# Decode attention that streams a 512 MiB K/V cache: V tiles moved to a second DMA queue, and one shared pool of buffers at the end

## The chip, the cores and the metric

One core of one Trainium2 chip runs the kernel. The metric is device time in microseconds (us), as the median of several executions. Executions of one kernel agree within about 0.1%, so differences of 2 us are readable. Profiled executions give a span that is about 1.8 us shorter than the device time of the same run (1308.8 us beside 1310.64 us for the kernel before). Times inside a trace count from the start of the span.

In the profile lines PE is TensorE, DVE is VectorE, ACT is ScalarE and SP is SyncE; SPq and ACTq are the parts of SyncE and ScalarE that issue loads. "The 16 engines" are the DMA engines that move the bytes. A load is issued when its instruction runs, and has landed when the last engine has counted up the load's semaphore. The PV product is softmax(scores) times V; an eviction is ScalarE's copy of its result from the buffer `psb` to `O_sb`.

## The reference, cut to what matters

Eight requests (B = 8) decode one token each. A gated mixture of two branches is computed:

```python
q = (x @ wq) per head                       # H = 32 heads, Dh = 128
scores = q . k_cache * Dh**-0.5             # k_cache: [8, 32, 4096, 128] bf16
o = softmax(scores) . v_cache               # v_cache: the same shape
a = o @ wo                                  # [4096, 576]
b = gelu(layernorm(x) @ w1 + b1) @ w2 + b2  # w1: [576, 4608], w2: [4608, 576]
out = g * a + (1 - g) * b                   # g: a sigmoid gate
```

The two caches are 268 MB each and every byte is read once. The four weights add 20 MB. The arithmetic on each byte is small, so this is a kernel that streams memory. The diffs and listings below are cut to their core: `...` and words in place of operands stand for what is left out.

## The kernel before

The work is cut into 64 tiles g: four heads of one request, K and V of 4 MiB each, 32 KB per partition. There are two buffers for K and two for V. One buffer `RB` holds the weights in turn: wq, then w1, then w2, then wo. Everything large is loaded from SyncE's queue, in program order:

```python
def load_k(g):                              # waits until the multiplies of tile g-2 have read the buffer
    k_land[g] = op("sync", dma KB[g % 2] <- k_cache tile g, [k_done.get(g - 2)], dma=(sK[s], ...))

def load_v(g):                              # waits until the PV product of tile g-2 has read the buffer
    t = op("sync", dma VB[g % 2] <- v_cache tile g, [v_done.get(g - 2)], dma=(sV[s], ...))
# (both abbreviated)

for g in range(NG):                         # NG = 64
    if 1 <= g <= NG - 3:
        load_k(g + 1)
    if 1 <= g <= NG - 2 and g != NG - 3:
        load_v(g)
    ...
    scores(g, between)                      # 4 chunks: VectorE multiplies K by q, TensorE sums, VectorE reduces
                                            # in chunk 3: the PV product of tile g-1 on TensorE, ScalarE evicts it
    if g == NG - 3:
        load_k(g + 2)
        load_v(g)
    ...
    if g == UP0 + UPN:  load_w2()           # g = 15; w1 is issued before the loop
    if g == DN0 + DNN:  load_wo()           # g = 25
    ...
    softmax(g)                              # ends in 4 exponentials on ScalarE
```

A K buffer is free after the fourth multiply of its tile (line `DVE p L354` in the profile). A V buffer is free one tile later, after the PV product (`PE psb L414`). The last V tile (V63) is loaded in seven pieces so that its product can start early.

## Time and profile before

| | before |
|---|---|
| median device time | 1310.35 us (3 runs, 1310.23 to 1310.52) |
| bytes moved by DMA | 557.8 MB |
| DMA rate in a steady stretch (620 to 1000 us) | 431 GB/s |
| VectorE, TensorE, ScalarE busy | 66%, 64%, 16% of the span |
| K load, issue to landing (median) | 27.2 us |
| V load, issue to landing (median) | 33.1 us |

These lines are from the profile page of the kernel before: the GB/s moved in each of 40 equal slices of the span, the main row of the DMA queue table (packets, MB, share of 16 engines' span), the chain of waits that ended last, the group of K multiplies on VectorE, and two rows of the list of DMA issues (count, KB each, us to landing).

```profile
GB/s 398 422 431 432 431 432 431 432 431 430 434 424 432 430 431 429 428 418 432 429 431 429 431 431 431 431 432 430 432 430 431 431 431 429 432 431 432 429 420 311
...
q1 hardware_dynamic: 24944, 556.95, 99.4%
...
DMA 69%; DVE 20%; PE 10%; SPq 0%; issue 0%; ACT 0%
...
L354 DVE TENSOR_TENSOR p<-KB,q_bc 128x4096 bf16<-128x4096 bf16 x256 | 579.6, 2285 | 278.0 <-DMA KB<-in_A_k_cache_dram 278.0
...
KB<-in_A_k_cache_dram SPq DMA_DIRECT2D x64, 4096.0 KB, 27.2
VB<-in_A_v_cache_dram SPq DMA_DIRECT2D x63, 4096.0 KB, 33.1
```

What to see: the rate is 429 to 434 GB/s in nearly all slices, queue 1 alone keeps the 16 DMA engines busy for 99.4% of the span, the chain is 69% DMA, and VectorE spent 278 us waiting for K tiles. This kernel is bound by its DMA engines. In the trace's packet records a 32 KB packet takes 1216 ns, and 16 engines at 32 KB per 1216 ns are the 431 GB/s. The Trainium skill, "DMA: Bandwidth & Descriptors", section "Where 436 GB/s comes from", gives 435.2 GB/s as the ceiling; this trace runs 1% below it.

### The profile page before, as it was taken

The numbers are of one execution on the slowest core, as the hardware profiler recorded it, in microseconds if no ns is written. First come the engines' busy times: TensorE is split into PE (matmuls) and PEld (weight loads), VectorE is DVE, ScalarE is ACT, GpSimd is POOL, SyncE is SP. The second block draws the span as 40 slices with busy tenths as digits, with TensorE's granted clock in tenths as the row PEclk, the third lists the DMA queues.
The fourth block names the chain that finished last, engine by engine and source line by source line (L and its number), as shares of the span: only waits on it lengthen the run. The fifth ranks groups of instructions, "written<-read, shape, count | busy, mean of one in ns | idle before, by whom it ended". The sixth has DMA issues, their size and how long they took to land.

```text
span 1308.8 us, 12641 instructions
## 1 busy us (share of the span) xinstructions
PE 843.5 (64%) x5428; PEld 384.4 (29%) x5428; DVE 869.7 (66%) x1061; ACT 204.1 (16%) x393; POOL 2.5 (0%) x13
## 2 busy tenths in 40 slices
PE   3567766766746666646766766765766665766766
PEld 1223433433312233212322222322322222322323
DVE  4576676676747667646766766766776666776675
ACT  1201111111210110101011111011111111111111
POOL 0000000000000000000000000000000000000000
PEclk8878888878868888768878878878878878878878
DMA  9999999999999999999999999999999999999997
GB/s 398 422 431 432 431 432 431 432 431 430 434 424 432 430 431 429 428 418 432 429 431 429 431 431 431 431 432 430 432 430 431 431 431 429 432 431 432 429 420 311
DMA packets 25255, 557.77 MB, mean 426 GB/s; under 512 B 2528, under 2 KB 6640, under 8 KB 7536
## 3 DMA queue, kind: packets, MB, share of 16 engines
q1 hardware_dynamic: 24944, 556.95, 99.4%
q8 instruction: 42, 0.69, 0.2%
q14 instruction: 13, 0.11, 0.0%
q10 hardware_dynamic: 256, 0.03, 0.0%
HBM read 556.96 MB, written 0.01 MB: 426 GB/s over the span
## 4 chain that ended last, share of the span: by engine, by line
DMA 69%; DVE 20%; PE 10%; SPq 0%; issue 0%; ACT 0%
DMA KB<-in_A_k_cache_dram 68%; DVE p L354 16%; PE psb L364 10%; DVE s_sb L369 3%; DMA VB<-in_A_v_cache_dram 1%; SPq L187 0%; PE psb L414 0%; ACT L467 0%; SPq L229 0%; DVE mA L387 0%; SPq L223 0%; PE psb L477 0%; DVE mB L389 0%; ACT O_sb L427 0%; DVE gm L390 0%
## 5 line engine op out<-in xcount | busy, mean ns | idle before, releaser
L364 PE MATMUL psb<-p,ident 128*128 128x512 bf16 x2048 | 610.9, 459 | 412.2 <-DVE p L354 411.8
L354 DVE TENSOR_TENSOR p<-KB,q_bc 128x4096 bf16<-128x4096 bf16 x256 | 579.6, 2285 | 278.0 <-DMA KB<-in_A_k_cache_dram 278.0
L364 PEld LDWEIGHTS psb<-p,ident 128*128 128x128 bf16 x2048 | 218.1, 114 | 744.5 <-DVE p L354 445.2
L369 DVE TENSOR_REDUCE s_sb<-psb 128x32 f32<-128x512 f32 x256 | 176.1, 688 | 129.9 <-PE psb L364 129.6
L427 ACT ACTIVATE O_sb<-psb 128x512 f32<-128x512 f32 x63 | 37.6, 597 | 1032.2 <-PE psb L414 1032.2
L396 ACT ACTIVATE P<-s_sb,mD 32x128 bf16<-32x128 f32 x256 | 147.0, 574 | 12.9 <-DVE mD L393 9.0
L414 PE MATMUL psb<-VB,P 128*16 128x512 bf16 x2016 | 119.9, 379 | 0.3 <-DMA VB<-in_A_v_cache_dram 0.3
L432 PE MATMUL psb<-sel,O_sb 128*128 128x4 f32 x504 | 66.9, 256 | 32.9 <-ACT O_sb L427 32.9
L432 PEld LDWEIGHTS psb<-sel,O_sb 128*128 128x128 f32 x504 | 61.6, 192 | 41.3 <-ACT O_sb L427 41.2
L414 PEld LDWEIGHTS psb<-VB,P 128*16 128x16 bf16 x2016 | 44.7, 89 | 70.4 <-issue 26.3
L402 DVE TENSOR_REDUCE rs<-P 128x4 f32<-128x512 bf16 x64 | 43.5, 680 | 2.1 <-ACT P L396 2.1
L421 PEld LDWEIGHTS psb<-rs,ones 128*128 128x128 f32 x128 | 24.4, 192 | 9.3 <-issue 0.4
L348 ACT ACTIVATE q_bc<-psb 128x128 bf16<-128x128 f32 x64 | 17.4, 272 | 32.7 <-PE psb L346 32.7
L452 PEld LDWEIGHTS psb<-yT_sb,RB 128*128 128x128 bf16 (+1 forms) x216 | 19.4, 165 | 3.4
L452 PE MATMUL psb<-yT_sb,RB 128*128 128x8 bf16 (+1 forms) x216 | 19.8, 227 | 0.0
L387 DVE TENSOR_REDUCE mA<-s_sb 128x1 f32<-128x128 f32 x64 | 18.3, 286 | 2.2
L421 PE MATMUL psb<-rs,ones 128*128 128x4 f32 x128 | 18.4, 214 | 0.0
L389 DVE STREAM_TRANSPOSE mB<-mA 128x32 f32<-128x32 f32 x64 | 13.6, 213 | 2.2
L393 DVE STREAM_TRANSPOSE mD<-mC 128x32 f32<-128x32 f32 x64 | 13.6, 212 | 2.2
L346 PE MATMUL psb<-Q,Sel 128*128 128x128 bf16 x64 | 14.7, 229 | 0.0
L346 PEld LDWEIGHTS psb<-Q,Sel 128*128 128x128 bf16 x64 | 6.1, 96 | 27.0 <-issue 26.8
L390 DVE TENSOR_REDUCE gm<-mB 128x1 f32<-128x32 f32 x64 | 11.9, 186 | 2.2
(63 smaller groups left out, 84.7 us busy)
## 6 DMA issues: line engine op xcount, KB each, us to landing
KB<-in_A_k_cache_dram SPq DMA_DIRECT2D x64, 4096.0 KB, 27.2
VB<-in_A_v_cache_dram SPq DMA_DIRECT2D x63, 4096.0 KB, 33.1
RB<-in_B_w_dram SPq DMA_DIRECT2D x1, 5184.0 KB, 44.3
RB<-in_B_w_dram SPq DMA_DIRECT2D x1, 4608.0 KB, 36.6
RB<-in_A_wo_dram SPq DMA_DIRECT2D x1, 4608.0 KB, 44.7
RB<-in_A_wq_dram SPq DMA_DIRECT2D x1, 4096.0 KB, 12.8
VB<-in_A_v_cache_dram SPq DMA_DIRECT2D x2, 1024.0 KB, 8.7
VB<-in_A_v_cache_dram SPq DMA_DIRECT2D x3, 512.0 KB, 11.2
```

Of the source, the lines that this page charges most:

```text
L346: t = op("tensor", lambda e: e.matmul(qb_ps[:, 0:DH], lhsT=Sel[:, b, :], rhs=Q4[:, hg * DH:(hg + 1) * DH], start=True, stop=True), [a_Q[hg ...
L354: v_mult[g, c] = op("vector", lambda e: e.tensor_tensor(out=p1[:, par, :, :], in0=KB[s][:, c * CT:(c + 1) * CT, :], in1=qb, op=ALU.mult), ...
L364: p_sum[g, c] = op("tensor", lambda e, r=r, n=n: e.matmul(tr_ps[par][:, :], lhsT=ident[:, :], rhs=r, start=(n == 0), stop=(n == NCH - 1)), w)
L369: v_red[g, c] = op("vector", lambda e: e.tensor_reduce(out=s_sb[:, s, c * CT:(c + 1) * CT], in_=tr_ps[par][:, :].rearrange("p (t c) -> p t ...
L387: t = op("vector", lambda e: e.tensor_reduce(out=mA[:, 0:1], in_=s_sb[:, s, :], axis=AX.X, op=ALU.max), [v_red[g, NCK - 1], c_mA])
L396: a_exp[g] = op("scalar", lambda e, h=h, q=q: e.activation(out=P[q, s, :, h], in_=s_sb[q, s, :], func=ACT.Exp, bias=mD[q, s, 0:1], scale=1.0),
L402: v_rs[g] = op("vector", lambda e: e.tensor_reduce(out=rs[:, s, :], in_=P[:, s, :, :].rearrange("p t h -> p h t"), axis=AX.X, op=ALU.add), ...
L414: p_pv[g] = op("tensor", lambda e, o=o, tq=tq: e.matmul(o, lhsT=P[:, s, tq * TQ:(tq + 1) * TQ, :].rearrange("p t h -> p (t h)"), rhs=VB[s] ...
L421: p_z[g] = op("tensor", lambda e: e.matmul(oz_ps[:, HB:2 * HB], lhsT=ones[:, :], rhs=rs[:, g % 2, :], start=True, stop=True), [v_rs[g], v_ ...
L427: a_ev[g] = op("scalar", lambda e: e.activation(out=O_sb[:].rearrange("p t d -> p (t d)"), in_=o_ps[s][:, :], func=ACT.Copy), [p_pv[g], p_ ...
L432: p_oz[g] = op("tensor", lambda e, tt=tt: e.matmul(oz_ps[:, 0:HB], lhsT=O_sb[:, tt, :], rhs=sel16[:, tt, :], start=(tt == 0), stop=(tt == ...
L452: st["p_up"] = op("tensor", lambda e, w=w, o=o, kt=kt: e.matmul(o, lhsT=w, rhs=yT_sb[:, kt, :], start=(kt == 0), stop=(kt >= NKF)), [*ld_w ...
```

## The change

Its intent: let a V and a K tile be in flight together from two queues, so that one queue's wait for a free buffer never holds up the other, and bring V63 and K63 forward at the end by letting them use whichever of the four buffers is free first. The diff, cut to its core:

```diff
-    KB = [sb(f"KB{i}", [128, NTT, DH], BF16) for i in range(2)]
-    VB = [sb(f"VB{i}", [128, NTT, DH], BF16) for i in range(2)]
+    KV = [sb(f"KV{i}", [128, NTT, DH], BF16) for i in range(4)]
...
+    k_slot = {g: g % 2 for g in range(NG)}
+    v_slot = {g: 2 + g % 2 for g in range(NG)}
+    k_slot[NG - 1], v_slot[NG - 3], v_slot[NG - 1] = 3, 1, 0
+    free = [None] * 4
...
+    def load_tile(cache, g, i, engine="sync"):
+        nS[i] += 1
+        src = kv_src(cache, g)
+        return op(engine, lambda e: e.dma_start(KV[i][:, :, :], src), [free[i]], dma=(sS[i], 16 * nS[i]))
...
     def load_v(g):
-        ... op("sync", ...)
+        v_land[g] = [(load_tile(A_v_cache, g, v_slot[g], "scalar" if 1 <= g < NG - 4 else "sync"), 0, NTT)]
...
     for g in range(NG):
         if 1 <= g <= NG - 3:
             load_k(g + 1)
+        if g == NG - 3:
+            load_k(g + 2)
+        if g == NG - 1:
+            load_v_pieces(g)
...
-                    pv(NG - 3, 0, 1)         # before: the pieces of V63 had to wait for this product
-                    evict(NG - 3)
-                    load_v_pieces(g)
```

So V1 to V59 are issued by ScalarE, in its program order after the exponentials of the tile before. The weights, K and the other V tiles stay on SyncE's queue.

More of the change, by code (lines that the diff above doesn't have):

```diff
@@ L180, in bass_gated_mix__mha_block_cached__mixer_channel_mlp__decode_kernel @@
     YT_COL = 64
-    sK = [nc.alloc_semaphore(f"sK{i}") for i in range(2)]
-    sV = [nc.alloc_semaphore(f"sV{i}") for i in range(2)]
-    nK, nV = [0, 0], [0, 0]
+    sS = [nc.alloc_semaphore(f"sS{i}") for i in range(4)]
+    nS = [0] * 4
+    k_slot = {g: g % 2 for g in range(NG)}
+    v_slot = {g: 2 + g % 2 for g in range(NG)}
+    k_slot[NG - 1], v_slot[NG - 3], v_slot[NG - 1] = 3, 1, 0
+    free = [None] * 4
     def load(engine, dst, src, name, waits=()):
@@ L214, in kv_src @@
         return cache[b, hg * HB:(hg + 1) * HB].rearrange("h (p t) d -> (h p) t d", p=32)
-    k_done, v_done = {}, {}
     k_land, v_land = {}, {}
+    def load_tile(cache, g, i, engine="sync"):
+        nS[i] += 1
+        src = kv_src(cache, g)
+        return op(engine, lambda e: e.dma_start(KV[i][:, :, :], src), [free[i]], dma=(sS[i], 16 * nS[i]))
     def load_k(g):
-        s = g % 2
-        nK[s] += 1
-        src = kv_src(A_k_cache, g)
-        k_land[g] = op("sync", lambda e: e.dma_start(KB[s][:, :, :], src), [k_done.get(g - 2)], dma=(sK[s], 16 * nK[s]))
+        k_land[g] = load_tile(A_k_cache, g, k_slot[g])
     def load_v(g):
-        s = g % 2
-        nV[s] += 1
-        src = kv_src(A_v_cache, g)
-        t = op("sync", lambda e: e.dma_start(VB[s][:, :, :], src), [v_done.get(g - 2)], dma=(sV[s], 16 * nV[s]))
-        v_land[g] = [(t, 0, NTT)]
+        v_land[g] = [(load_tile(A_v_cache, g, v_slot[g], "scalar" if 1 <= g < NG - 4 else "sync"), 0, NTT)]
     V_LAST = (32, 32, 16, 16, 16, 8, 8)
     def load_v_pieces(g):
-        s = g % 2
+        i = v_slot[g]
         src = kv_src(A_v_cache, g)
@@ L239, in load_v_pieces @@
         for n, nt in enumerate(V_LAST):
-            dst, part = VB[s][:, t0:t0 + nt, :], src[:, t0:t0 + nt, :]
-            t = load("sync", dst, part, f"sVl{n}", [v_done.get(g - 2)])
+            dst, part = KV[i][:, t0:t0 + nt, :], src[:, t0:t0 + nt, :]
+            t = load("sync", dst, part, f"sVl{n}", [free[i]])
             v_land[g].append((t, t0, t0 + nt))
@@ L354, in mult @@
         v_mult[g, c] = op("vector", lambda e: e.tensor_tensor(
-            out=p1[:, par, :, :], in0=KB[s][:, c * CT:(c + 1) * CT, :], in1=qb, op=ALU.mult),
+            out=p1[:, par, :, :], in0=KV[k_slot[g]][:, c * CT:(c + 1) * CT, :], in1=qb, op=ALU.mult),
             [k_land[g], a_qb[g], p_sum.get((g, c - 2) if c >= 2 else (g - 1, c + NCK - 2))]
@@ L358, in mult @@
         if c == NCK - 1:
-            k_done[g] = v_mult[g, c]
+            free[k_slot[g]] = v_mult[g, c]
         for n in range(NCH):
@@ L415, in pv @@
                     o, lhsT=P[:, s, tq * TQ:(tq + 1) * TQ, :].rearrange("p t h -> p (t h)"),
-                    rhs=VB[s][:, tq * TQ:(tq + 1) * TQ, :].rearrange("p t d -> p (t d)"),
+                    rhs=KV[v_slot[g]][:, tq * TQ:(tq + 1) * TQ, :].rearrange("p t d -> p (t d)"),
                     start=(tq < 4), stop=(tq >= NTQ - 4)), w)
-        v_done[g] = p_pv[g]
+        free[v_slot[g]] = p_pv[g]
     def total(g):
@@ L508, in pv_turned @@
                 p_oz[g] = op("tensor", lambda e, t=t: e.matmul(
-                    o_ps[s][:, 0:HB], lhsT=VB[s][:, t, :], rhs=P[:, s, t, :], start=(t == 0), stop=(t == NTT - 1)),
+                    o_ps[s][:, 0:HB], lhsT=KV[v_slot[g]][:, t, :], rhs=P[:, s, t, :], start=(t == 0), stop=(t == NTT - 1)),
                     [land, a_exp[g], a_ev.get(g - 2)] if t == t0 else ())
@@ L539, in between @@
                     total(g - 1)
-                else:
-                    pv(NG - 3, 0, 1)
-                    evict(NG - 3)
-                    load_v_pieces(g)
             if c == 2:
@@ L555, in between @@
                     evict(g - 1)
+                if g == NG - 1:
+                    pv(g - 2, 0, 1)
+                    evict(g - 2)
                 if g == UP0 + UPN:
@@ L562, in bass_gated_mix__mha_block_cached__mixer_channel_mlp__decode_kernel @@
         if g == NG - 3:
-            load_k(g + 2)
             load_v(g)
```

## The prediction

> **What bounds it.** The DMA engines. The DMA queue table gives queue 1 556.95 MB and 99.4% of the 16 engines' span; the 40-slice strip shows DMA at 9 throughout and 429 to 432 GB/s in almost every slice; the chain of waits is 68% K loads. In the packet records a 32 KB packet takes 1216 ns (middle half 1214 to 1219), i.e. 16 x 26.95 GB/s = 431 GB/s: packets follow each other without gaps. VectorE (66%) and TensorE (64%) have room: in a pair's 19.45 us of DMA, the last multiply ends 11.7 us after its K landed.
>
> The Trainium skill, "DMA: Bandwidth & Descriptors", "Where 436 GB/s comes from", puts the ceiling at 435.2 GB/s; the trace agrees, being 1% below it. So even a perfect rate over 557 MB could save only about 12 us (estimate from that page's figure).
>
> **What the change does.**
> 1. 59 V loads (V1 to V59) move from SyncE's queue to ScalarE's. By the page's "Issuing engines are not separate DMA queues" both run on the same 16 engines. No byte and no gap between packets is there to be removed: I expect 430 to 433 GB/s in steady stretches: 0 us, perhaps -4.
> 2. ScalarE issues 59 loads at 0.33 us = 19 us, on an engine 16% busy: off the path. A V load now follows the four exponentials of the previous tile, about 3 us later than its buffer is free. At half rate a V tile takes 19.45 us, so the next V is queued before the last lands: both queues stay filled.
> 3. Transients. Where SyncE's queue holds weights ahead of K (w1 at 45 to 60 us, w2 near 330, wo near 540), V no longer waits behind them and runs two tiles ahead, worst at wo, whose 1152-byte packets (51 ns) alternate with V's 1216 ns packets if engines switch per packet. Afterwards K streams alone at 9.7 us a tile, faster than the 11.7 us that free a K buffer: 1 to 4 us of DMA idleness each, estimate +5 us in all.
> 4. End. Now V63 waits for the PV product of tile 61 and is issued at 1289.5 us; the windows view shows 360, 221, 291 GB/s in 1286 to 1292 us (about 2 us of DMA time lost). With the pool, V63 goes into K62's buffer, free about 13 us earlier, so the gap disappears: -2 to -3 us. The tail after the last landing (about 4.1 us) stays.
>
> All DMA time, and nothing else, is on the critical path. Sum: +5 -2.5 -1.5 = +1 us. I predict **1310 us, range 1301 to 1319** (8 in 10); chances: faster by over 2% 0.03, within 2% 0.93, slower 0.04.
>
> **What would show it.** Right: queue 1 about 309 MB and queue 10 about 247 MB, summing in time to nearly the whole span; steady windows at 431 GB/s; K's median issue-to-landing still about 27 us, V's up from 33 to 36 to 40 us; no dip below 380 GB/s before the last 8 us; short dips near 95, 350 and 575 us; VectorE still waiting for K about 4 us per tile. Step 1 is wrong if steady windows leave 429 to 434; step 3 is wrong if those dips are absent; step 4 if the last 25 us still dip.
>
> **What would make it wrong.** Two interleaved streams could cost the HBM side rate (a steady 5 GB/s less is +15 us); sharing could be unfair per queue, so that K, which gates the multiplies, lands later and starves VectorE; or SyncE's blocked issue (23.6 us once, near 542 us, behind wo) could hold up ScalarE's issue and with it the exponentials.

## The result, and the profile after

The changed kernel takes 1322.97 us (median of 4 runs, 1322.59 to 1323.56), beside 1310.40 us for the kernel before in the same rounds. The ratio is 1.0096, 95% interval 1.0079 to 1.0114. A ratio here is the mean time of one kernel's runs over that of the other's of the same rounds, so it is not quite the ratio of the medians. The change made the kernel 12.6 us slower. That is within 2%, and outside the predicted range.

The same lines of the profile page, of the changed kernel (queue 10 is ScalarE's):

```profile
GB/s 398 423 373 419 435 429 427 432 434 431 434 425 392 429 428 434 432 409 365 432 436 430 428 428 436 432 431 429 431 429 431 434 430 432 429 429 433 431 434 306
...
q1 hardware_dynamic: 16448, 309.48, 54.9%
q10 hardware_dynamic: 8752, 247.50, 43.6%
...
DMA 56%; DVE 23%; PE 14%; another core or an unknown queue 6%; ACT 1%; issue 0%; SPq 0%; DVEq 0%
...
L354 DVE TENSOR_TENSOR p<-KV,q_bc 128x4096 bf16<-128x4096 bf16 x256 | 579.6, 2285 | 295.5 <-DMA KV<-in_A_k_cache_dram 289.3
...
KV<-in_A_k_cache_dram SPq DMA_DIRECT2D x64, 4096.0 KB, 27.2
KV<-in_A_v_cache_dram ACTq DMA_DIRECT2D x59, 4096.0 KB, 28.0
```

Most slices still show 427 to 435 GB/s. The lost time is local: apart from the first slices and the last, which are alike in both, slices 3 and 4 (373 and 419), 13 (392) and 18 and 19 (409 and 365) lie below the rest, where the kernel before has 431, 432, 432, 418 and 432.

The windows view shows what happens there. Its columns are the window, its length, busy time and instruction count of each engine, the granted clock, the DMA share and the GB/s. First the kernel before, then the changed one:

```profile
60.00:100.00 40.00, 22.90 (x129) 11.34 (x130) 25.06 (x26) 5.90 (x12) 0.00 (x0) 0.79 1.00 430
380.00:420.00 40.00, 26.28 (x156) 11.64 (x155) 27.74 (x33) 6.12 (x12) 0.00 (x0) 0.82 1.00 428
600.00:640.00 40.00, 25.84 (x182) 11.50 (x182) 27.15 (x33) 6.13 (x12) 0.00 (x0) 0.84 1.00 429
620.00:1000.00 380.00, 249.40 (x1508) 109.10 (x1509) 263.31 (x312) 58.21 (x114) 0.00 (x0) 0.82 1.00 431
```

```profile
60.00:94.00 34.00, 5.72 (x22) 2.71 (x22) 6.38 (x8) 3.02 (x6) 0.00 (x0) 0.55 1.03 438
94.00:99.00 5.00, 3.19 (x16) 1.43 (x15) 5.00 (x4) 0.00 (x0) 0.00 (x0) 1.00 0.05 20
99.00:104.00 5.00, 4.46 (x48) 2.18 (x47) 2.66 (x8) 1.39 (x4) 0.00 (x0) 1.00 0.89 321
402.00:408.00 6.00, 3.96 (x20) 1.83 (x19) 5.37 (x4) 0.00 (x0) 0.00 (x0) 1.00 0.69 257
614.00:620.00 6.00, 4.92 (x21) 2.04 (x19) 5.60 (x4) 0.00 (x0) 0.00 (x0) 0.87 0.13 55
700.00:1200.00 500.00, 327.67 (x1973) 143.48 (x1973) 345.47 (x410) 76.54 (x150) 0.00 (x0) 0.82 1.00 431
```

In three short stretches the changed kernel moves far less than in the others: 20 GB/s from 94 to 99 us, 257 GB/s from 402 to 408 us, 55 GB/s from 614 to 620 us. Elsewhere the rate is 431 GB/s over 500 us, as before. From the packet records, the time in which the 16 engines had no packet sums (as a mean over engines) to about 4.7, 2.6 and 4.7 us in the three stretches, 12.0 us together (12.2 us if the first and last moments of each stretch are counted in full); the kernel before has none there. At the end (from 1255 us to the last packet) the engines idle for 7.2 us after and 7.0 us before. The 12.0 us are nearly the whole difference between the two profiled spans (1321.7 - 1308.8 = 12.9 us). The median duration of a 32 KB packet is unchanged (1216 ns before; 1215 ns on either queue after), so two streams side by side cost no rate that can be seen.

Why the first stretch is idle can be read from the timeline of the changed kernel (start us, duration, engine and line, operation, count, and in brackets the idle time before and what ended it). These are the K multiplies of tile 2 and the next issues of V (ScalarE) and of K (SyncE):

```profile
56.15 0.33 SPq L224 DMA_DIRECT2D KV<-in_A_k_cache_dram  x1
```

```profile
60.12 0.33 ACTq L224 DMA_DIRECT2D KV<-in_A_v_cache_dram  x1
...
102.73 0.34 ACTq L224 DMA_DIRECT2D KV<-in_A_v_cache_dram  x1
```

```profile
87.06 4.50 DVE L354 TENSOR_TENSOR p<-KV,q_bc 128x4096 bf16<-128x4096 bf16 x2 [27.00 <-DMA KV<-in_A_k_cache_dram]
...
93.65 2.28 DVE L354 TENSOR_TENSOR p<-KV,q_bc 128x4096 bf16<-128x4096 bf16 x1
...
96.45 2.28 DVE L354 TENSOR_TENSOR p<-KV,q_bc 128x4096 bf16<-128x4096 bf16 x1
```

```profile
98.76 0.33 SPq L224 DMA_DIRECT2D KV<-in_A_k_cache_dram  x1
```

K3 was issued at 56.15 us, V2 at 60.12 us. VectorE then waited 27 us for K2, which lay in SyncE's queue behind w1, while V used the other queue: K2 landed at 87.0 us (in the kernel before, VectorE started on it at 67.9 us), and V2 had landed at 76.4 us, before it. From there both V buffers were full, and V3 could only be issued at 102.73 us, after the PV product of tile 1. So only K3 was left to move. With the engines to itself it took about 10 us and its last packet ended at 96.3 us. The next K load needs the buffer of K2, which VectorE had read by 98.76 us. Its first packet ran at 99.7 us. In between the DMA engines had nothing to do. The same pattern follows w2 and wo. After wo it is as strong: both V buffers were full at 594.5 us, the held K tile landed at 607.2 us, and the next K load was issued at 619.1 us. After w2 it is milder: the last V tile landed at 401.9 us, 6.4 us after the held K tile (395.4 us), so V had not got as far ahead. The next K load was issued at 406.8 us, before the K tile ahead of it had wholly landed (407.9 us), and the engines ran dry one after another from 404 us on; all 16 were without a packet for only 0.3 us, against 3.4 us in the first stretch and 3.6 us in the third.

### The profile page after: what moved, and what is told of

The parts are those of the page before. It is cut to its first block, busy times and chain, and to the rows that moved or that the text cites. A ratio compares the mean times of both kernels' runs of the same rounds, so it can differ in the third digit from the quotient of the medians.

```text
span 1321.7 us, 12641 instructions
## 1 busy us (share of the span) xinstructions
PE 836.4 (63%) x5428; PEld 381.3 (29%) x5428; DVE 869.5 (66%) x1061; ACT 204.2 (15%) x393; POOL 2.5 (0%) x13
## 4 chain that ended last, share of the span: by engine, by line
DMA 56%; DVE 23%; PE 14%; another core or an unknown queue 6%; ACT 1%; issue 0%; SPq 0%; DVEq 0%
DMA KV<-in_A_k_cache_dram 56%; DVE p L354 19%; PE psb L364 12%; DVE s_sb L369 4%; PE psb L414 2%; ACT O_sb L427 0%; PE psb L508 0%; ACT q_bc L348 0%; PE psb L432 0%; SPq L190 0%; ACT L467 0%; SPq L224 0%; DVE mA L387 0%; DVE rs L402 0%
## 5 line engine op out<-in xcount | busy, mean ns | idle before, releaser
L354 DVE TENSOR_TENSOR p<-KV,q_bc 128x4096 bf16<-128x4096 bf16 x256 | 579.6, 2285 | 295.5 <-DMA KV<-in_A_k_cache_dram 289.3
L414 PE MATMUL psb<-KV,P 128*16 128x512 bf16 x2016 | 119.9, 379 | 0.0
L414 PEld LDWEIGHTS psb<-KV,P 128*16 128x16 bf16 x2016 | 44.7, 89 | 69.9 <-issue 26.3
```

The costliest lines, as they stand in the source:

```text
L354: v_mult[g, c] = op("vector", lambda e: e.tensor_tensor(out=p1[:, par, :, :], in0=KV[k_slot[g]][:, c * CT:(c + 1) * CT, :], in1=qb, op=ALU ...
L414: p_pv[g] = op("tensor", lambda e, o=o, tq=tq: e.matmul(o, lhsT=P[:, s, tq * TQ:(tq + 1) * TQ, :].rearrange("p t h -> p (t h)"), rhs=KV[v_ ...
```

## The experiments

Eleven kernels were run, each timed against the kernel before in 3 rounds on the same chip. All results passed the comparison with the reference, even that of the one kernel that uses wrong rows of wo (the comparison did not notice it). "Idle" below is the mean time without a packet over the 16 engines, worked out from the packet records of the trace, in stretches apart from the start and the end.

### Which part of the change costs: the second queue or the new end?

Only the queue of V is changed in the kernel before:

```diff
-        t = op("sync", ...VB[s]..., [v_done.get(g - 2)], ...)
+        t = op("scalar" if 1 <= g < NG - 4 else "sync", ...VB[s]..., [v_done.get(g - 2)], ...)
```

> The kernel before, with one thing changed: V1 to V59 are issued from ScalarE's queue. The order at the end and the buffers stay as they were. Theory (V runs two tiles ahead while weights sit in SyncE's queue, then K alone drains its queue before a K buffer is free): the three idle stretches of the DMA engines near 95, 405 and 615 us appear as in the changed kernel, 12 us together, and the time is 1321 to 1324 us. Rival (the new order at the end, with K63 in a V buffer and V63 in a K buffer, is what costs): within 2 us of the kernel before.

Measured: 1323.23 us, ratio 1.0098 (1.0083 to 1.0113). Idle: 4.8, 3.2 and 4.9 us at the same three places.

Only the new end is kept:

```diff
-        ... "scalar" if 1 <= g < NG - 4 else "sync"
+        ... "sync"
```

> The changed kernel with every load on SyncE's queue again, so only the rearranged end of the change is left. Theory: no idle stretch outside the end; 1307 to 1311 us, since the end of the changed kernel lost as much DMA time (7.2 us) as that of the kernel before (7.0 us). Rival (the end costs): above 1315 us.

Measured: 1310.31 us, ratio 0.9999 (0.9982 to 1.0016), no idle stretch. The three windows of the kernel with only the queue changed show the idle stretches without the new end:

```profile
94.00:98.00 4.00, 3.99 (x16) 1.63 (x14) 4.00 (x3) 0.00 (x0) 0.00 (x0) 0.84 0.04 16
404.00:408.00 4.00, 2.43 (x11) 0.99 (x12) 4.00 (x4) 0.00 (x0) 0.00 (x0) 1.00 0.23 98
615.00:619.00 4.00, 2.91 (x15) 1.28 (x12) 4.00 (x3) 0.00 (x0) 0.00 (x0) 1.00 0.15 66
```

The queue costs the 12.6 us, and the end neither costs nor gains.

### Is it V running ahead, or are two streams the trouble?

V stays on ScalarE's queue, and waits one event more:

```diff
+        after_k = [k_land[g]] if engine == "scalar" else []
-        return op(engine, ..., [free[i]], ...)
+        return op(engine, ..., [free[i], *after_k], ...)
```

> The changed kernel, and each V load on ScalarE's queue also waits until the K tile of the same number has landed, so V cannot run ahead of K while weights are loaded. Both queues still run together. Theory: the three idle stretches are gone or below 1 us each, 1309 to 1312 us. Rival (two interleaved streams cost by themselves, or issuing late from ScalarE starves the DMA engines): as slow as the changed kernel, 1320 us or more, since V is now issued later still.

Measured: 1310.33 us, ratio 0.9998 (0.9983 to 1.0013). The windows that were idle are full:

```profile
94.00:98.00 4.00, 2.49 (x10) 1.14 (x10) 4.00 (x2) 1.89 (x4) 0.00 (x0) 0.66 0.96 406
404.00:408.00 4.00, 3.48 (x14) 1.57 (x13) 3.97 (x6) 0.00 (x0) 0.00 (x0) 0.76 0.95 410
615.00:619.00 4.00, 3.27 (x29) 1.43 (x30) 3.53 (x4) 0.00 (x0) 0.00 (x0) 1.00 1.02 442
```

Two queues are in use as before, and V is issued later than in the changed kernel, and still the loss is gone. So neither interleaving nor a late issue from ScalarE is the cause. The loss comes from the order in which tiles arrive: it is gone when V may not run ahead of K.

### Does it matter which stream the weights hold up?

```diff
-    ld_w1 = [load("sync", w1_sb, ...), load("sync", w1_t, ...)]
+    ld_w1 = [load("scalar", w1_sb, ...), load("scalar", w1_t, ...)]
     # likewise w2 and wo
```

> The changed kernel with w1, w2 and wo loaded from ScalarE's queue, ahead of V instead of ahead of K. Theory: K is no longer held up, so the stretches near 95 and 405 us vanish (7.3 us less); wo may block ScalarE itself, as it blocked SyncE's next issue for 35 us, and that would stop the exponentials, so its stretch may stay or grow. 1310 to 1320 us. Rival (the loads of weights cost the same wherever they are queued, because two queues share the engines): 1322 us with three stretches.

Measured: 1310.42 us, ratio 0.9999 (0.9984 to 1.0014), no idle stretch, not even the one after wo that the expectation left open. With the weights ahead of V it is V that comes late, and V has slack: a tile's product is needed only near the end of the next tile's multiplies. The feared block did occur, and cost nothing. The timeline of ScalarE in this run, around wo:

```profile
551.98 0.39 ACTq L190 DMA_DIRECT2D RB<-in_A_wo_dram  x1
...
552.52 31.87 ACTq L224 DMA_DIRECT2D KV<-in_A_v_cache_dram  x1
...
584.43 0.60 ACT L427 ACTIVATE O_sb<-psb 128x512 f32<-128x512 f32 x1 [29.49 <-issue]
```

The V load behind wo held ScalarE's queue for 31.87 us, and the eviction at 584.43 us came 29.49 us after ScalarE's last work. Enough K and V was in the queues that the DMA engines did not run dry.

### Is a whole K buffer the wait that leaves the engines idle?

V may run ahead here, but K is loaded and freed in halves:

```diff
+        k_half[g] = op("sync", dma first half of K,  [half_free[i]], dma=(sH[i], ...))   # free after multiply 1
+        k_land[g] = op("sync", dma second half of K, [free[i]], dma=(sS[i], ...))        # free after multiply 3
```

> The changed kernel with each K tile loaded as two halves of 2 MiB, each half waiting only for the multiplies that read it. V still runs ahead as in the changed kernel. The first half of a K buffer is free about 4.6 us after its K landed, sooner than the other K buffer is filled by K alone (about 8 us after). Theory (the idle stretch is K waiting for a whole buffer): no stretch over 1 us; the halves double K's packets, estimated from 32 KB at 1216 ns and 8 KB at 309 ns as 3 us more in all, so 1312 to 1315 us. Rival (V running ahead is harmful in itself, whatever K's grain): stretches as before, 1324 us or more.

Measured: 1315.06 us, ratio 1.0034 (1.0019 to 1.0049), at the top of the expected range (0.06 us above it), with no idle stretch (426, 422 and 475 GB/s in the windows at 94 to 98, 404 to 408 and 615 to 619 us). V did run ahead here: V2 landed at 83.4 us, K2 at 87.5 us. The remaining 4.5 us (against 1310.57 us for the kernel before in these rounds) fit the smaller packets: a 16 KB packet takes 614 ns, so two take 12 ns more than one of 32 KB, and the packet time summed over the run is 5.8 us per engine above that of the changed kernel (1310.2 against 1304.4 us), which more than covers them. Two things are needed for the idle stretch, then: V has run ahead, and K waits for a whole buffer. Taking away either one removes it.

### Does the size of packets decide how far V gets ahead?

wo is read as one run of 36 KB per partition, which puts the wrong rows in it (a wrong result):

```diff
-        A_wo.rearrange("(h d) n -> d h n", d=128)     # 32 runs of 1152 B per partition
+        A_wo.rearrange("(d h) n -> d h n", d=128)     # 1 run of 36 KB per partition
```

> The changed kernel with wo read as one run of 36 KB per partition in place of 32 runs of 1152 bytes: wrong result on purpose, same bytes. If the engines switch between the queues packet by packet, V is held up by wo as it is by w2 (41 KB packets, stretch 2.6 us), and the third stretch shrinks from 4.7 us to 2 to 3.5 us; with 2 us less for the larger packets the time is 1318 to 1320 us. Rival (the size of the stretch does not come from the packets' sizes): the stretch stays at 4.7 us and the time at 1320.5 to 1321.5 us.

Measured: 1319.47 us, ratio 1.0067 (1.0051 to 1.0084). The third stretch shrank from 4.7 to 2.2 us; the first stayed near 4.7 us and the second was 3.2 us:

```profile
94.00:98.00 4.00, 2.89 (x15) 1.28 (x12) 4.00 (x3) 0.00 (x0) 0.00 (x0) 1.00 0.04 16
612.00:618.00 6.00, 4.86 (x26) 2.08 (x28) 4.61 (x4) 0.00 (x0) 0.00 (x0) 1.00 0.67 240
```

The packet records show why. In the changed kernel, from 584 to 592 us, 111 packets of wo and 111 packets of V were started, and each of the 111 of wo lay directly between two of V (within 6 ns): the engines alternate one for one, and with 1152 bytes against 32 KB that gives V 97% of the bytes. With wo in 36 KB packets, 53 of wo stand beside 50 of V from 572 to 580 us, and the last V tile before the stretch landed at 609.2 us in place of 594.5 us, so K streamed alone for a shorter time. (The run changes one more thing: the K load behind wo was issued in 0.33 us, where it held SyncE's queue for 35.4 us in the changed kernel. The two K tiles behind wo landed at 604.3 and 616.4 us, against 607.2 and 616.9 us, so it is V's lead that changed most.) The Trainium skill, "DMA: Bandwidth & Descriptors", section "Queues, rings and completion order", says that each engine goes round its queues packet by packet; this agrees. It also gives 9 to 17 descriptors as a typical packet; in these records the turn changes after every single run of bytes.

### Does one more weight load in K's queue make one more idle stretch?

wo is loaded a second time (the same bytes) during tile 40, with its readers moved behind it; in the changed kernel, and as a control in the kernel with all loads on SyncE's queue:

```diff
-    AP0 = 28
+    AP0 = 50
...
+        if g == 40:
+            st["ld_wo"] = load("sync", wo_sb, ..., "ld_wo2", [st["ld_wo"]])
```

> The changed kernel with wo loaded once more (same bytes) on SyncE's queue during tile 40, all its readers moved behind that. Theory: a fourth idle stretch of 4 to 5 us appears near 900 to 930 us, beside the 13 us that the bytes take: 1339.5 to 1341.5 us. Rival (the stretches come from what is special at 95, 405 and 615 us, such as the projections on TensorE, and not from the load in K's queue): no fourth stretch, 1335.5 to 1336.5 us.

> The control of the run before: the same second load of wo in the kernel with every load on SyncE's queue. All theories: no idle stretch, the bytes alone, 13 us more than that kernel: 1322.5 to 1324.5 us.

Measured: 1340.10 us, ratio 1.0226 (1.0210 to 1.0241), for the changed kernel, and 1322.42 us, ratio 1.0090 (1.0075 to 1.0105), for the control. The same window of the two runs, changed kernel first:

```profile
924.00:930.00 6.00, 4.49 (x20) 1.92 (x18) 5.75 (x5) 0.00 (x0) 0.00 (x0) 0.90 0.13 55
```

```profile
924.00:930.00 6.00, 2.87 (x7) 1.03 (x8) 5.18 (x5) 0.06 (x1) 0.00 (x0) 0.50 0.99 426
```

The control pays 12.1 us for the bytes (1322.42 - 1310.31), a little less than the 13 us expected. The changed kernel pays 17.1 us (1340.10 - 1322.97), and has a fourth idle stretch of 5.7 us at a time of our choosing. (The numbers in each difference come from different rounds, in which the kernel before differs by 0.1 to 0.2 us.) The stretches come from the load in K's queue, and not from what else happens at those times.

### Why did the new end gain nothing?

The kernel with only the new end is the test, and here are its last windows beside those of the kernel before (before first):

```profile
1286.00:1292.00 6.00, 5.61 (x50) 2.15 (x49) 6.00 (x5) 0.60 (x1) 0.00 (x0) 1.00 0.72 291
1292.00:1296.00 4.00, 3.67 (x40) 2.18 (x42) 2.26 (x9) 0.38 (x1) 0.00 (x0) 1.00 0.96 395
1296.00:1302.00 6.00, 4.84 (x101) 4.32 (x94) 1.19 (x4) 2.52 (x5) 0.00 (x0) 0.76 1.00 394
1302.00:1305.00 3.00, 2.07 (x57) 1.74 (x54) 0.04 (x1) 0.00 (x0) 0.00 (x0) 0.50 0.19 70
```

```profile
1286.00:1292.00 6.00, 4.59 (x18) 1.61 (x16) 5.76 (x5) 0.00 (x0) 0.00 (x0) 0.87 1.01 425
1292.00:1296.00 4.00, 3.73 (x40) 1.40 (x40) 2.30 (x7) 0.22 (x1) 0.00 (x0) 1.00 0.96 389
1296.00:1302.00 6.00, 5.57 (x115) 4.43 (x115) 1.41 (x5) 3.31 (x6) 0.00 (x0) 1.00 0.58 236
1302.00:1305.00 3.00, 2.38 (x72) 2.07 (x68) 0.36 (x2) 0.00 (x0) 0.00 (x0) 0.94 0.14 49
```

The dip at 1286 to 1292 us (291 GB/s) is gone (425), and in its place the engines run at 0.58 of their number from 1296 to 1302 us (236 instead of 394 GB/s). The last piece landed at 1304.7 us before and at 1304.4 us with the new end. A load of 128 partitions counts up its semaphore 16 times in the trace, once for each engine; the first and the last of these counts for that last piece are 2.6 us apart before and 8.4 us with the new end. So in the kernel before, engines that were ahead stood idle in the dip while the slow ones still worked, and the slow ones set the end in both. In the kernel before, this distance grows from 0.5 us for the first tile to 7.7 us for the tile that landed at 1235 us. It grows in steps: one engine counts 1.5 us or more after the first engine for the load that landed at 56.7 us, two at 106.7 us, three at 135.9 us and five at 165.4 us. By those times one, two, three and five fetches of instructions in packets of 16 KB had passed over the same engines (the first at 52.7 us, about 1.1 us each; in all 55 fetches of 0.80 MB, queues 8 and 14 of the queue table), and 32 KB packets that take 1.6 to 1.9 us instead of 1.22 stand at the times of the fetches. So the fetches are the likely reason; no run took them away to test it.

Two runs tried to test this by moving work between engines, and did not succeed. The last quarter of V63 was loaded in groups of 8 partitions, which by a rule of the Trainium skill ("DMA: Bandwidth & Descriptors", section "Why a DMA increments its semaphore by 16 and not by 1") use only the 8 lowest-numbered engines:

```diff
+            if t0 >= NTT - 32:
+                for r in range(0, 128, 8):
+                    op("sync", dma rows r..r+8 of the piece, [free[i]], dma=(sem, 16))
+                t = ("dma", sem, 16 * 16)
```

> The control with the rearranged end on one queue, whose end gap is gone at no gain. Its last 32 of 128 V rows per partition (1 MiB, 2.4 us on 16 engines) are now loaded in groups of 8 partitions, which by the skill's rule run on the 8 lowest-numbered engines only, so these 8 carry 2.4 us more each and the other 8 carry 2.4 us less. Theory (the end waits for the slowest DMA engines, which never idled in the gap, while the first engine ends over 7 us sooner): the time moves by more than 1 us, to about 1308 us if the slowest engines are among the upper 8, to 1312 or 1313 us if among the lower 8. Rival (the engines end together and the end is bound by arithmetic or by all engines alike): the lower 8 would all end 2.4 us late, so also 1312 to 1313 us; a time of 1308 us therefore speaks for the theory, 1312 us for neither, and 1310 us against both.

Measured: 1318.52 us, ratio 1.0062 (1.0045 to 1.0079). It is outside every expectation. The 48 issues held SyncE's queue from 1278.4 to 1304.7 us, so the run cannot be read as a test of the engines. The second try made one piece of the last quarter, 16 issues, with a control that has the four pieces alone:

> Control for the next run: the rearranged end on one queue, with the last V tile loaded in four equal pieces of 1 MiB in place of seven. The last piece now needs 32 matmuls after it lands in place of 8, about 0.7 us more: 1310.5 to 1311.5 us under every theory.

> The same, with the last of the four pieces loaded as 16 transfers of 8 partitions each, which by the skill's rule use the 8 lowest-numbered engines only: those carry 2.4 us more, the others 2.4 us less, and the 16 issues (about 0.55 us each in the failed run before) are over by 1290 us, so they cannot bound it as they did there. Theory (a few slow engines end over 7 us after the first and alone set the end): 1308 to 1309.5 us if the slow ones are among the upper 8, 1313 to 1314 us if among the lower 8. Rival (all engines end alike): 1313 to 1314 us too. Below the control speaks for the theory; above it leaves both.

Measured: control 1310.83 us, ratio 1.0002 (0.9985 to 1.0018), as expected; with the groups 1316.52 us, ratio 1.0044 (1.0029 to 1.0059), more than either theory gave. The 16 issues were over at 1283.6 us this time. All 16 groups count up one semaphore, so a count cannot be told to its group, but the trace has 144 counts: 16 at the times of the issues, and eight more for each group. Of these 128 counts 80 had come by 1303.1 us. The last 48, as many as three engines give for 16 groups, came between 1304.4 and 1310.3 us, when no more than about three packets were under way at a time and an 8 KB packet took 309 ns, as in the control. So in this run a few engines that were behind set the end, while the others idled. (In the control, 7 engines had counted the last piece by 1297.1 us and the other 9 between 1302.3 and 1304.3 us.) A second thing made the run slower than expected: from 1294 to 1300 us, while the groups and the other pieces ran side by side, the median 8 KB packet took 475 to 509 ns, against 309 to 313 ns in the control. Its cause is open. Which engines are slow stays open too, and no run made the end earlier by relieving them, so that they alone set the end of the kernel before is argued and not proven. That the dip was not on the path is shown, as its removal changed nothing.

### Is there a version that beats both?

None of those that were run does. The three versions without idle stretches on 32 KB packets (1310.31, 1310.33 and 1310.42 us) equal the kernel before to within 0.2 us, although their queues differ. At 431 GB/s and 557 MB little else is left. If two queues are wanted, the V wait of one line or the weights on V's queue makes them harmless.

## Why the prediction was wrong

It said 1310 us, 1301 to 1319; measured was 1322.97 us. Point by point:

- **What bounds the kernel** was right. Nearly all time lost (12.0 of 12.9 us) is time in which DMA engines are idle.
- **Step 1, the rate**: 430 to 433 GB/s was expected, and 431 GB/s measured. The allowance of -1.5 us in the sum was worth 0.
- **Step 2, steady stretches**: no gap appears there, so both queues do stay supplied. V's issue to landing was expected to rise to 36 to 40 us and fell to 28.0 us: a V tile is issued about 10 us before the V ahead of it lands (V issued at 154.99 us, the V tile ahead landed at 164.7 us and this one at 184.1 us). I had overrated the backlog; it did no harm. K's 27 us were right. Nor is V issued 3 us after its buffer is free: most V loads are issued 0.16 us after the eviction of the product that frees the buffer has begun, and before the exponentials run, which were only ahead of it in program order (60.12 us against 59.96 and 60.75 us for V2).
- **Step 3, the transients**, is the step that failed, and by its size. The mechanism was right: V runs ahead at w1, w2 and wo, then K streams alone faster than it is freed, and dips appear near 95, 405 and 615 us (predicted near 95, 350 and 575 us, so two came 40 to 55 us later than said). The term "1 to 4 us of DMA idleness each, estimate +5 us in all" measured 4.7 + 2.6 + 4.7 = 12.0 us. I took 9.7 us of streaming from the 11.7 us that free a buffer and so got about 2 us. But the two do not start together: K3's packets follow K2's at once, while the 11.7 us start only when K2's landing is signalled (87.0 us, where K2's packets had ended at 86.3 us); the next K is issued at 98.76 us and its first packet runs at 99.7 us; and engines that end early or start late add to the mean. So the idle time is nearer 5 than 2 us. "Worst at wo" was also wrong: w1 in packets of 9 KB and wo in packets of 1152 bytes cost the same, 4.7 us. V has two buffers and can get no further ahead than that, and in both cases it got there, with the second V tile landed 10.7 us (w1) and 12.7 us (wo) before the held K tile; at w2, in 41 KB packets, its second tile landed 6.4 us after K's, and the cost was less.
- **Step 4, the end**: -2.5 us expected, 0 measured. The dip was there, but I read a mean over 16 engines as time on the path. By the counts above, the engines that were idle in it were those that were ahead, and its removal (425 in place of 291 GB/s) left the time at 1310.31 us.
- **The sum**: +5 - 2.5 - 1.5 should have read +12 + 0 + 0. The two gains were both unproven, and they hid a loss that I had seen.
- **The list of signs** contradicted itself: it asked for no dip below 380 GB/s and for short dips at three places. The dips came, to 20, 257 and 55 GB/s.
- **SyncE's blocked issue** (23.6 us before) grew to 35.4 us behind wo and cost nothing by itself: all idle time there is in the stretch after it, and the kernel with the same block on ScalarE lost nothing.

## What to carry to other kernels

When the DMA engines are already full, a second queue brings no bytes (431 GB/s here with one queue and with two), but it does give up the order of one queue, and with it the guarantee that the tile needed next comes next. Look for a large load that sits in one queue only: the other stream then fills its buffers, stops, and the held stream alone must keep the engines busy, which it can only do if its buffers come free faster than it fills them (here 11.7 us to free one against 9.7 us to fill the other). Tie the free-running stream to the other's progress by one wait, or put the large load into the queue that has slack; and before counting a dip in a mean rate as a gain, ask whether the engine that ends last was idle in it.

## What the Trainium skill lacked or had wrong

- "DMA: Bandwidth & Descriptors", section "Issuing engines are not separate DMA queues", says that issuing from several engines only saves issue time. The rate part agrees (431 GB/s with one queue and with two). It lacks that splitting can cost time through the lost order: 12.6 us of 1310 here, with three stretches of 4.7, 2.6 and 4.7 us without DMA.
- The same page, section "Queues, rings and completion order", gives 9 to 17 descriptors as a typical packet between changes of queue. Here the engines changed after every run of bytes, 111 packets of 1152 bytes each between two of 111 packets of 32 KB, so a load in small runs gets 3% of the bytes beside a load in large ones.
- The same page does not mention that a load of many small runs can make the next issue block the issuing engine: 23.6 us (SyncE, before), 35.4 us (SyncE, after) and 31.9 us (ScalarE, with the weights there), each behind wo with its 4096 runs of 1152 bytes. With wo in 128 runs of 36 KB the issue behind it took 0.33 us.
- No page that I read says that the 16 engines drift apart over a long stream: the first and the last engine's count for one tile were 0.5 us apart at the start and 7.7 us apart near the end, with 55 instruction fetches (0.80 MB) on the same engines. That the fetches are the cause was not tested. (The Trainium skill, "DMA: Bandwidth & Descriptors", section "Latency and other measured facts", calls engines 7 and 15 usually slower. Here nine of the 16 were 5.5 us or more behind the first for the load that landed at 1225.5 us; the trace does not name the engine of a packet, so no run shows which.)
- The rule of "DMA: Bandwidth & Descriptors", section "Why a DMA increments its semaphore by 16 and not by 1", by which 8 partitions use the 8 lowest-numbered engines, agrees in the number: 16 such loads gave 16 counts at the issues and 128 later, eight for each. Which eight engines they were, the trace does not name.
